# Mean and variance of the first four row tiles: ScalarE running totals replaced by VectorE statistics passes, with ten preparatory products and a new order

## The chip, the cores and the metric

The kernel runs on one core of one Trainium2 chip. The metric is device time in microseconds (us). The time before is 519.17 us, the median of three runs (518.96 to 519.18). All times of the text are us of one execution that the hardware profiler took, unless they are called run times.

## What is computed

x has 2048 rows of 512 columns, all fp32. With xn the layer norm of x along its columns:

```python
def _A_ref(x, wqkv, wo):                     # linear attention, 32 heads of 16
    q, k, v = split(x @ wqkv)
    phi = lambda t: where(t > 0, t + 1, exp(t)) + 1e-6
    kv, z = sum over rows of phi(k) v^T and of phi(k)
    return (phi(q) kv / (phi(q) z + 1e-6)) @ wo

def _B_ref(x, w1, w2, w3, w4):               # a token mixer, then an MLP of width 1376
    h = gelu(layernorm(x) @ w1)
    hs = (four column quarters of h, shifted by +1, -1, +2, -2 rows) @ w2
    x1 = x + hs
    return x1 + gelu(layernorm(x1) @ w3) @ w4

xn = layernorm(x)
out = x + _A_ref(xn, wqkv, wo) * silu(_B_ref(xn, w1, w2, w3, w4))
```

## The kernel before

The rows are 16 tiles of 128 (NT), in four blocks of four tiles (QT = 4). Most fp32 products are made on TensorE from two rounded parts of each operand, a high part (names that end in h) and the rest (names in l): three products hi*hi, lo*hi, hi*lo take the place of one. ScalarE (ACT) copies the high part, VectorE (DVE) subtracts it from the full value for the rest. A few products run in plain fp32, each as two passes: the preparatory ones (`warm`), the first chunk of the first two k tiles (`raw_k`), the column sums `ksum` and `qsum`, and the small kv and m products.

The work goes through these stages. (1) Load wk, the transposed x of block 0 (xt, u) and the four row tiles x0 to x3; make k of the tiles 0 to 3, their phi (`feature_k`: kt, kr, kNh, kNl), q of the same tiles (`query`), and the sum over rows of k times x, called g (`gram`). (2) The same for the later tiles, with the mixer of the block before between them. (3) kv and m (what attention multiplies q by). (4) The MLP, block by block: products a, pa, pb, pe, then acc, with the attention products pas, pbs, pes between, and at the end the gate and the stores.

The products of x itself do not wait for the norm: k and q are made from the raw x, and the mean is taken out afterwards with `wneg` and `qneg` (minus the column sums of the weights), the scale by rs1 = 1/sqrt(var + eps). So the mean and variance of tile i, held in `mv1`, are needed by `feature_k(i)` (the mean, in kt on VectorE), by `query(i)` (qt), and by `scale_x` (line 598): four small GpSimd (POOL) instructions w, rs (L596, a power), ns, nm, after which ACT normalises x in place (`x<-x,nm,rs`) and x is split into xNh and xNl for `gram(i)`.

How mv1 is made is `load_rows(i)` (line 1175). For tiles 4 to 15 it calls `moments` (line 588): one statistics pass of VectorE over the 512 columns (BATCH_NORM_STATS2, L590) and a short aggregate (L591). For tiles 0 to 3 it uses ACT: a copy of x with a running total (`sq<-x`), two VectorE instructions on one column that turn the total into the mean and its negative, a second ACT pass (`sq<-x,sx`, the squares of x minus the mean, with a running total), and one more VectorE instruction on one column that divides. Each running total is read out by an ACTIVATION_READ_ACCUMULATOR.

The order of the instructions on each engine isn't that of the source. `Plan` (line 86) records every operation with planned durations. `deadlines` (line 240) gives each TensorE product a nominal time and every other operation a due time, counted back from its consumers (`backward`, line 261); an operation that touches PSUM may be due no later than PATIENCE us after it could run. `nudged` (line 234) makes single operations due earlier by 0.25 times the number beside them in the table SOONER (line 1401). `emit` (line 267) then places operation after operation in a planned time line, the one that is due first among those that can go, and lets TensorE take products out of turn within `window`. Buffers come from pools: `p` with 90 tiles, `mm` and `acc` with four PSUM banks each; `lead` and `reserve` say how early an operation may take a buffer. Each engine runs its own list strictly in the planned order; where a planned time doesn't hold on the chip, the engine waits.

The helpers through which all instructions go give the line numbers of the profile: matmul L146, ACT L167, VectorE and GpSimd two-operand L189, one-operand L194, scalar-tensor-tensor L199; loads from SP L205, stores L210 and L212, fetches L217, accumulating DMAs from POOL L223. PE is TensorE, PEld its weight loads.

Of the kernel before, what the change touches and what calls it, by code (L numbers as in the profile page):

```python
# [10 lines left out]
AF = mybir.ActivationFunctionType  # L11
ALU = mybir.AluOpType
# [73 lines left out]
class Plan:  # L86
# [138 lines left out]


    GAP = .06
    PATIENCE = 2.5
    COLD, COLD_TILL = 1.84, 5.8
    SAFE = 2.0  # L230
    early = 0.0
# [8 lines left out]
    def deadlines(self, first):  # L240
# [8 lines left out]
        for op in self.ops:  # L249
# [3 lines left out]
            elif any(t.psum for t in op.tiles):  # L253
                op.due = min(op.due, op.at + self.PATIENCE)
            elif op.soon:
# [5 lines left out]
    def backward(self):  # L261
        for op in reversed(self.ops):
            if op.eng != "PE":
                for o in op.post:
                    op.due = min(op.due, o.due - self.GAP - (6.0 + op.mb * 4 if op.mb else op.lat))

    def emit(self, first, lead, reserve, window, ahead, table=()):
        self.deadlines(first)
# [125 lines left out]
def linear_attn_gated_by_mixer(  # L394
# [14 lines left out]
    S, D = x.shape  # L409
# [5 lines left out]
    QT = 4  # L415
# [3 lines left out]
    W = 4  # L419
    SHIFT = (-1, 1, -2, 2)  # L420
    ORDER = (0, 2, 1, 3)
    WARM = 8
    PIECE = BT + W
    EARLY = (), ()
    AHEAD = 30.0, 20.0, 10.0, 0.0, 0.0
# [12 lines left out]
    pl = Plan(nc, pools, counts, ("acc", "mm"))  # L438

    def piece(name, dt=F32):  # L440
        return pl.new("p", name, dt, PIECE)[:, :512]
# [8 lines left out]
    def bank(name):  # L450
        return pl.new("mm", name, F32, 512)[:, :]
# [81 lines left out]
    X, XT = {}, {}  # L533

    def load_x(i):
        X[i] = piece(f"x{i}")
        pl.load(X[i], x[i * P:(i + 1) * P, :])
# [47 lines left out]
    def small(name, n):  # L585
        return pl.new("sm", name, F32, n)

    def moments(name, xv, mv):
        st = small(name, 6).all
        pl.add("DVE", .62, .69, [xv], [st], lambda: nc.vector.bn_stats(st.get(), xv.get()))  # L590
        pl.add("DVE", .12, .2, [st], [mv], lambda: nc.vector.bn_aggr(mv.get(), st.get()))  # L591
# [576 lines left out]
    warm = bank("warm")  # L1168
    for n in range(WARM):
        pl.mm(warm.cols(n % NC * P, (n % NC + 1) * P), ones.all, ones.all, True, True, slow=True)  # L1170
# [4 lines left out]
    def load_rows(i):  # L1175
        load_x(i)
        mv = mv1[:, 2 * i:2 * i + 2]
        if i >= QT:
            moments(f"st{i}", X[i], mv)
            return  # L1180
        t, m, v = piece(f"sq{i}"), mv.cols(0, 1), mv.cols(1, 2)
        s = small(f"sx{i}", 2).all
        pl.act(t, X[i], AF.Copy, total=s.cols(0, 1))
        pl.ts(m, s.cols(0, 1), 1.0 / D, None, ALU.mult)
        pl.ts(s.cols(1, 2), s.cols(0, 1), -1.0 / D, None, ALU.mult)
        pl.act(t, X[i], AF.Square, bias=s.cols(1, 2), total=v)
        pl.ts(v, v, 1.0 / D, None, ALU.mult)

    WK = Weights("wk", wqkv[1])
    load_u(0, 2)  # L1190
# [1 line left out]
    for i in range(QT):  # L1192
        load_rows(i)
# [26 lines left out]
    query(1)  # L1220
    load_u(1, 1)
    load_rows(QT)
    scale_x(QT, 1)
    gram(1)
# [11 lines left out]
    for b in range(1, NQ):  # L1236
# [8 lines left out]
        for j in range(b == 1, QT):  # L1245
            load_rows(t0 + j)
# [50 lines left out]
    for base, s in ((0, 1), (DH - 1, -1)):  # L1297
        v = bmask.all.via(lambda ap: ap.rearrange("p (h d) -> p h d", d=DH))
# [35 lines left out]
    for b in range(NQ):  # L1334
# [46 lines left out]
        else:  # L1381
# [3 lines left out]
            t = piece(f"xi{i}", F32R)  # L1385
# [13 lines left out]
                gate(b * QT + QT - 1, a, o, D // 2, late=True, by_dma=False, whole=o > 0)  # L1399

    SOONER = (
# [6 lines left out]
    )  # L1408
    pl.emit(first=6.0, lead={"p": 14.0, "w": 14.0, "ab": 10.0}, reserve={"p": 20, "w": 1, "ab": 0}, window=12.0,
            ahead=6.0, table=SOONER)  # L1410


# [35 lines left out]
```

## Time and profile before

| | us |
|---|---|
| run time, median of three runs | 519.17 |
| run time of the profiled execution | 519.35 |
| its span, first to last instruction | 517.6 |
| PE busy | 511.2 (99%) |
| DVE busy | 394.0 (76%) |
| ACT busy | 324.8 (63%) |
| POOL busy | 102.8 (20%) |

The span is shorter than the run time by 1.75 us. Matmuls are pipelined: one of 512 columns is on record for about 0.39 us, and the next starts about 0.23 us after it, so that two overlap and the engine counts as busy without being stopped by anything. Where TensorE waits, the start of a product stands later behind the start of the one before than this step. A row of the timeline has the start, the duration, the engine, the line, the operation with output<-inputs, and the count of merged instructions; the idle time before it stands in brackets with what ended it.

### The profile page before, as it was taken

Reading aid. Unit: us, or ns where it says so; the run is one execution under the profiler, and the core shown is the slowest. Engines: PE = TensorE matmul, PEld = TensorE weight load, DVE = VectorE, ACT = ScalarE, POOL = GpSimd, SP = SyncE. Lnnn points to the kernel's source line nnn. Section 1 sums busy time; section 2 is a strip of 40 time slices with the busy share of each in tenths; the row PEclk is TensorE's granted clock in tenths of the full one; section 3 lists DMA queues with packets and bytes.
Section 4 is the critical chain, followed back from the end, with each engine's and each line's share of the span. In section 5 each row is a group of like instructions: output and inputs, shape, how many; then the busy total and the mean of one; then the engine's idle time right before and its main releaser. Section 6 shows DMA issues by size and latency. Waiting matters only on the chain.

```text
span 517.6 us, 8927 instructions
## 1 busy us (share of the span) xinstructions
PE 511.2 (99%) x3005; PEld 445.0 (86%) x3005; DVE 394.0 (76%) x788; ACT 324.8 (63%) x664; POOL 102.8 (20%) x195
## 2 busy tenths in 40 slices
PE   8999999999999999999999999999999999999996
PEld 6777888988888888898889989899898898999985
DVE  5884987569567838999999999655886657895635
ACT  5899784579558657787866755345453545535621
POOL 1378643431363022211100001000020000200000
PEclk9999999999999999999999999999999999999999
DMA  8759994375976389989767759648488376687604
GB/s 277 255 101 248 225 205 97 74 172 182 220 169 162 68 185 249 259 261 262 287 200 225 237 175 249 212 152 208 133 214 276 122 201 157 179 248 225 243 1 122
DMA packets 73281, 100.12 MB, mean 193 GB/s; under 512 B 7844, under 2 KB 30900, under 8 KB 73236
## 3 DMA queue, kind: packets, MB, share of 16 engines
q1 hardware_dynamic: 63876, 82.52, 50.6%
q0 software_dynamic: 9360, 17.04, 19.9%
q8 instruction: 23, 0.38, 0.3%
q14 instruction: 22, 0.18, 0.1%
HBM read 60.33 MB, written 30.81 MB: 176 GB/s over the span
## 4 chain that ended last, share of the span: by engine, by line
PE 91%; ACT 5%; DVE 2%; DMA 1%; issue 1%; SPq 0%; DVEq 0%
PE acc L146 22%; PE pb L146 10%; PE k L146 8%; PE h L146 8%; PE q L146 7%; PE g L146 7%; PE pe L146 5%; PE pbs L146 5%; PE pbm L146 4%; PE pa L146 3%; PE pes L146 2%; PE a L146 2%; PE pem L146 2%; PE pas L146 1%; ACT y L167 1%; PE pam L146 1%
## 5 line engine op out<-in xcount | busy, mean ns | idle before, releaser
L223 POOL DMA_DIRECT2D th<-in_x x14 | 12.2, 919 | 247.3 <-PE a L146 126.2
L167 ACT ACTIVATE p<-pb 128x256 f32<-128x256 f32 x20 | 7.7, 385 | 25.8 <-PE pb L146 25.4
L223 POOL DMA_DIRECT2D o<-x x16 | 15.0, 935 | 40.4 <-DVE o L189 19.7
L223 POOL DMA_DIRECT2D zacc<-kr x16 | 14.6, 910 | 41.8 <-DVE kr L199 33.6
L167 ACT ACTIVATE th<-xo 128x512 f32<-128x512 f32 (+1 forms) x16 | 9.7, 619 | 19.3 <-DVE xo L189 16.2
L167 ACT ACTIVATE gf<-gf 128x512 f32<-128x512 f32 (+1 forms) x40 | 20.9, 523 | 0.8
L223 POOL DMA_DIRECT2D pqd<-qe x16 | 14.7, 921 | 28.9 <-ACT p5m L167 10.0
L167 ACT ACTIVATE p<-pe 128x256 f32<-128x256 f32 x20 | 7.7, 386 | 18.9 <-PE pe L146 18.9
L189 DVE TENSOR_TENSOR xo<-acc,xo 128x512 f32<-128x512 f32 (+1 forms) x16 | 10.3, 670 | 11.4 <-PE acc L146 11.4
L199 DVE SCALAR_TENSOR_TENSOR kt<-wneg,mv,k 128x512 f32<-128x512 f32 x16 | 11.9, 742 | 9.4 <-PE k L146 8.5
L199 DVE SCALAR_TENSOR_TENSOR kr<-kt,kr 128x512 f32<-128x512 f32 x16 | 11.0, 690 | 10.4 <-ACT kt L167 10.4
L199 DVE SCALAR_TENSOR_TENSOR qt<-qneg,mv,q 128x512 f32<-128x512 f32 x16 | 11.9, 742 | 7.2 <-PE q L146 7.1
L167 ACT ACTIVATE ht<-ht 128x512 f32<-128x512 f32 x16 | 10.0, 630 | 11.5 <-DVE ht L189 11.4
L189 DVE TENSOR_TENSOR gf<-u,pe 128x256 f32<-128x256 f32 x20 | 8.3, 416 | 11.2 <-PE pe L146 11.2
L189 DVE TENSOR_TENSOR gf<-pa,p 128x256 f32<-128x256 f32 x20 | 8.4, 418 | 10.5 <-PE pa L146 10.4
L189 DVE TENSOR_TENSOR ht<-h,abc 128x512 f32<-128x512 f32 x16 | 10.8, 686 | 6.5 <-PE h L146 6.5
L167 ACT ACTIVATE x<-x,nm,rs 128x512 f32<-128x512 f32 x16 | 12.5, 802 | 2.9 <-POOL nm L189 2.9
L167 ACT ACTIVATE qr<-qt,rs 128x512 f32<-128x512 f32 x16 | 11.4, 715 | 4.1 <-DVE qt L199 4.1
L590 DVE BATCH_NORM_STATS2 st<-o 128x6 f32<-128x512 f32 x16 | 10.9, 683 | 1.8 <-DMA o<-x 1.8
L167 ACT ACTIVATE kr<-kt,rs 128x512 f32<-128x512 f32 x16 | 11.4, 715 | 1.2 <-DVE kt L199 1.1
L167 ACT ACTIVATE y<-o,nm,rs 128x512 f32<-128x512 f32 x16 | 12.0, 805 | 0.1
L167 ACT ACTIVATE kt<-kt,rs 128x512 f32<-128x512 f32 x16 | 11.4, 715 | 0.1
(1559 smaller groups left out, 2195.9 us busy)
## 6 DMA issues: line engine op xcount, KB each, us to landing
w_s<-in_w SPq DMA_DIRECT2D x28, 256.0 KB, 5.5
x<-in_x SPq DMA_DIRECT2D x16, 256.0 KB, 5.2
zacc<-kr POOLq DMA_DIRECT2D x16, 256.0 KB, 3.9
pqd<-qr SPq DMA_DIRECT2D x16, 256.0 KB, 3.3
pqd<-qe POOLq DMA_DIRECT2D x16, 256.0 KB, 5.4
o<-x POOLq DMA_DIRECT2D x16, 256.0 KB, 4.6
x1d<-o SPq DMA_DIRECT2D x16, 256.0 KB, 4.9
pq<-pqd SPq DMA_DIRECT2D x16, 256.0 KB, 6.0
```

The lines of the kernel that those rows point to most:

```text
L146: lambda: nc.tensor.matmul(out.get(), lhs.get(), rhs.get(), start=start, stop=stop, skip_group_check=more))
L167: nc.scalar.activation(out.get(), src.get(), func, scale=get(scale), **kw)
L189: self.vec(eng, out, [a, b], lambda: self.e(eng).tensor_tensor(out.get(), a.get(), b.get(), op=op), True)
L199: lambda: self.nc.vector.scalar_tensor_tensor(out.get(), a.get(), get(s), b.get(), op0=op0, op1=op1),
L223: lambda: self.nc.gpsimd.dma_start(out.get(), get(src), accum_op=ALU.add), mb=mb)
L590: pl.add("DVE", .62, .69, [xv], [st], lambda: nc.vector.bn_stats(st.get(), xv.get()))
```

## The change

`load_rows` calls `moments` for all tiles: the eight ACT passes with running totals on tiles 0 to 3 and their twelve VectorE instructions on one column go, four statistics passes and four aggregates of VectorE come. WARM, the number of preparatory products, goes from 8 to 10. The planner's parameters are changed (PATIENCE, the time that a load is due ahead, the `lead` and `reserve` of the pool p, the `window` of TensorE), and SOONER is a new table. Together they give a new order on every engine.

```diff
-    PATIENCE = 2.5
+    PATIENCE = 6.0
...
-                    op.due = min(op.due, o.due - self.GAP - (6.0 + op.mb * 4 if op.mb else op.lat))
+                    op.due = min(op.due, o.due - self.GAP - (5.0 + op.mb * 4 if op.mb else op.lat))
...
-    WARM = 8
+    WARM = 10
...
         mv = mv1[:, 2 * i:2 * i + 2]
-        if i >= QT:
-            moments(f"st{i}", X[i], mv)
-            return
-        t, m, v = piece(f"sq{i}"), mv.cols(0, 1), mv.cols(1, 2)
-        s = small(f"sx{i}", 2).all
-        pl.act(t, X[i], AF.Copy, total=s.cols(0, 1))
-        pl.ts(m, s.cols(0, 1), 1.0 / D, None, ALU.mult)
-        pl.ts(s.cols(1, 2), s.cols(0, 1), -1.0 / D, None, ALU.mult)
-        pl.act(t, X[i], AF.Square, bias=s.cols(1, 2), total=v)
-        pl.ts(v, v, 1.0 / D, None, ALU.mult)
+        moments(f"st{i}", X[i], mv)
...
     SOONER = (
-        19, 20867, 20, 10505, 21, 8920, 22, 8153, 23, 20874, 26, 12597, 28, 17, 29, 8881, 34, 1005, 35, 11144,
...
+        21, 21467, 22, 10543, 23, 8942, 24, 8165, 25, 21457, 28, 13316, 30, 56, 31, 8859, 33, 37, 36, 1010,
...
-    pl.emit(first=6.0, lead={"p": 14.0, "w": 14.0, "ab": 10.0}, reserve={"p": 20, "w": 1, "ab": 0}, window=12.0,
+    pl.emit(first=6.0, lead={"p": 12.0, "w": 14.0, "ab": 10.0}, reserve={"p": 26, "w": 1, "ab": 0}, window=9.0,
             ahead=6.0, table=SOONER)
```

What the new order does, read from the two programs side by side:

- The products are the same but for the two more `warm`, and TensorE's order differs in a few places: `qsum` follows the twelve products of q0 in place of standing before the last two; g of tile 1 follows q1 directly, where it stood behind the first four products of q2; the three products for each of g's four column groups stand together for g1 and g2; near the first mixer products (profile time 91) products of q8 stand between them; one kv product goes ahead of the first six pem products of tile 12 that follow pbm, where it stood behind the second; the m products are in three runs in place of two; in stage 4, block 0, some acc products stand elsewhere between pas, pbs, pes, pb and pe. The last 150 products are in the same order.
- SP's first two loads change places (wk ahead of the first half of xt), the last part of xt comes ahead of x0, x1 moves up by two loads, and two loads for block 1 move back.
- ACT's list at the start: u2h, wk3h, u3h, wq3h, wq0h, wq2h, the normalising of x0, wneg, wq1h, x0h, then kr and kt of the tiles 0 and 1. Before, the normalising of x0 stood seven places behind wneg.
- VectorE's list: the statistics pass of x0 follows u3l, that of x1 follows wq3l; after wneg come kt0, kt1, wq1l, the statistics of x2, wqt, kr0, wqt (the last one that `qsum` needs), x0l, k0l.
- GpSimd's four instructions for x1 follow those for x0 at once; before, an accumulating DMA stood between.

13 rows, old and new, of the table SOONER are left out of this document.

## The prediction

> **What bounds the kernel now.** First the page: busy times of the engines and the chain of waits.
>
> ```profile
> PE 511.2 (99%) x3005; PEld 445.0 (86%) x3005; DVE 394.0 (76%) x788; ACT 324.8 (63%) x664; POOL 102.8 (20%) x195
> PE 91%; ACT 5%; DVE 2%; DMA 1%; issue 1%; SPq 0%; DVEq 0%
> ```
>
> TensorE is busy for 511.2 us, 99% of the span, and 91% of the chain that ended last is its products. So only three things can move the end: when the stream of products starts, how long it stands still in between, and the tail. "Busy" hides short waits, as products overlap on record; for those I read the steps between starts in the timeline. The undisturbed step comes from the chain of waits in order of time, the waits from the timeline of TensorE:
>
> ```profile
> 37.02 2.78 PE q L146 x12
> ...
> 18.30 0.39 PE L146 MATMUL q<-wq_0h,u_0h 128*128 128x512 f32 x1
> ...
> 22.11 0.40 PE L146 MATMUL g<-k0h,x0h 128*128 128x512 f32 x1
> ...
> 25.05 0.40 PE L146 MATMUL q<-wq_0h,u_0h 128*128 128x512 f32 x1
> ...
> 28.54 0.40 PE L146 MATMUL q<-wq_1h,u_1h 128*128 128x512 f32 x1
> 29.03 0.97 PE L146 MATMUL g<-k1h,x1h 128*128 128x512 f32 x3
> 29.83 0.63 PE L146 MATMUL g<-k1l,x1h 128*128 128x512 f32 x2
> ...
> 33.53 0.39 PE L146 MATMUL q<-wq_3h,u_3l 128*128 128x512 f32 x1
> 33.94 1.20 PE L146 MATMUL g<-k2h,x2h 128*128 128x512 f32 x4
> 34.98 0.40 PE L146 MATMUL g<-k2l,x2h 128*128 128x512 f32 x1
> ```
>
> Twelve products in 2.78 us are 0.232 us each. The twelve of g0 take 25.05 - 22.11 = 2.94, so 0.16 too long. From 28.54 to 29.03 is 0.49 for one product: 0.26 of waiting, and the three behind it take 0.80 in place of 0.70. From 33.53 to 33.94 is 0.41: 0.18, and the four behind take 1.04 in place of 0.93. **In all 0.16 + 0.36 + 0.29 = 0.81 us that TensorE waits for g's operands.** The busy time by stretches says who is late there (columns: PE, PEld, DVE, ACT, POOL busy):
>
> ```profile
> 20.00:40.00 20.00, 19.88 (x82) 14.77 (x81) 16.80 (x39) 20.00 (x37) 12.08 (x22) 1.00 0.51 101
> 260.00:280.00 20.00, 19.93 (x129) 17.79 (x128) 20.00 (x44) 12.83 (x30) 0.00 (x0) 1.00 0.68 211
> ```
>
> Between 20 and 40 ACT has no free time at all; between 260 and 280 it is VectorE that has none. The first is where the change takes work away, the second is where its new order is at risk.
>
> **The change part by part.** *ACT's passes.* The grouped lines of ACT from 9 to 28 us, and for the other side the page's row of statistics passes:
>
> ```profile
> L167 ACT ACTIVATE sq<-x,sx 128x512 f32<-128x512 f32 x4 | 2.8, 708 | 0.0
> L167 ACT ACTIVATE sq<-x 128x512 f32<-128x512 f32 x4 | 2.5, 618 | 0.0
> ...
> L590 DVE BATCH_NORM_STATS2 st<-o 128x6 f32<-128x512 f32 x16 | 10.9, 683 | 1.8 <-DMA o<-x 1.8
> ```
>
> ACT loses 2.8 + 2.5 = 5.3 us and the read-outs of the totals, all of it before 28 us. VectorE gains four passes of 0.68, 2.7 us, and four aggregates, and loses twelve instructions on one column; it has 3.2 us free between 20 and 40, so this is covered, unless it stands ahead of something that TensorE needs. In the new order g1 follows q1, so TensorE comes to it at about 28.1, 0.9 us sooner than before; following the new lists with the steps of the rows (0.60 for VectorE's 512 columns, 0.52 to 0.70 for ACT's), k1h ends near 25.4, k1l near 26.1, x1l near 26.8, so there is 1.3 us to spare. For g2 (33.6) k2h ends near 30.8, k2l and x2l near 31.8. I count all 0.81 us as gone; **-0.81**. Bounds: nothing, if the operands are late again, to -0.81.
>
> *Two more preparatory products.*
>
> ```profile
> 1.12 3.78 PE L146 MATMUL warm<-ones 128*128 128x128 f32 x16 [1.12 <-POOL ones L503]
> 5.27 2.60 PE L146 MATMUL k<-wk_s,xt 128*128 128x512 f32 x4 [0.37 <-DMA wk_s<-in_wqkv]
> ...
> 225.71 2.40 PE L146 MATMUL kv<-gs,wv_s 128*128 128x128 f32 x20
> ```
>
> Each product is two passes; 16 passes take 3.78 us with the last one's drain, about 0.215 from start to start. The same kind of pass takes 2.40 / 20 = 0.12 in the kv products: TensorE starts slow and becomes fast somewhere on the way; that the four k passes, four times as wide, go in 2.60 (0.65 each with the drain, not 0.86) puts this into their time. Four more passes take 0.86 us; the stream of `warm` then ends its issue near 5.55, past the 5.27 at which wk's landing let the first k product go. So that starts 0.28 later. Until the clock opens it runs at half speed, so what it does not do in that time costs half of it later: **+0.14**, between 0 (if data are later anyway) and 0.28. The exchange of the first two loads covers nothing: both are needed for the first k product.
>
> The gate's rule is in the Trainium skill, "TensorE: Matmul & The Clock Gate", Part 1: activity is counted in windows of 3.4 us that run freely, and one busy window opens the clock. By it, filling the 0.37 us of idle time opens nothing sooner, as the window that ended in the fast clock was busy enough with that gap. The rows agree with an opening within these four passes; where the windows lie in a run no row here can show.
>
> *The wait that is added.* In ACT's new list the normalising of x0 stands ahead of wneg, and it waits for GpSimd's nm of x0. Behind it in ACT's queue are wneg, wq1h and all of kr and kt; VectorE's kt0, wq1l and the last wqt wait for these, TensorE's `qsum` for that.
>
> ```profile
> 13.08 0.25 POOL L194 TENSOR_SCALAR w<-mv 128x1 f32<-128x1 f32 x1 [10.02 <-DVE mv L194]
> ...
> 15.22 0.47 POOL L189 TENSOR_TENSOR nm<-mv,ns 128x1 f32<-128x1 f32 x1
> ...
> 15.73 0.60 ACT L167 ACTIVATE wneg<-ksum 128x512 f32<-128x512 f32 x1 [1.58 <-PE ksum L146]
> ...
> 16.36 0.75 DVE L199 SCALAR_TENSOR_TENSOR kt<-wneg,mv,k 128x512 f32<-128x512 f32 x1 [0.72 <-ACT wneg L167]
> ```
>
> The chain on GpSimd takes 15.22 + 0.47 - 13.08 = 2.61. It started when mv was there, at 13.08. In VectorE's new list one pass (0.68) more stands ahead of that mv, but half a pass (u0l) and three short instructions fewer, and the load that u3 needs comes sooner: mv near 13.1 again, nm near 15.7. Normalising x0 then holds ACT for 0.70, wneg goes from 15.73 to 16.4, and kt0 from 16.36 to 17.0. Then VectorE has kt0, kt1 (0.66 each), wq1l, a statistics pass, wqt, kr0 (0.60 each) and the last wqt, which ends at 21.4. q0 starts at 18.30 + 0.14 and its twelve products end at 21.2, and `qsum` waits: **+0.25**. If GpSimd is as quick as its fastest rows, nothing; if mv is there one pass later, +0.9. I take the rows' own times.
>
> *Later places.* TensorE's other waits of that kind, from the timeline:
>
> ```profile
> 221.59 0.28 PE L146 MATMUL pbm<-w_t2h,hs23l 128*128 128x256 f32 x1
> 222.15 0.38 PE L146 MATMUL pem<-w_b22h,hs43h 128*128 128x256 f32 x1 [0.28 <-ACT p5m L167]
> ...
> 262.83 0.40 PE L146 MATMUL acc<-w_1l,f_1h 128*128 128x512 f32 x1
> 263.30 0.39 PE L146 MATMUL pb<-yt40h,w_b 128*128 128x256 f32 x1
> ```
>
> At 221.59 one product of 256 columns (step 0.12) takes 0.56: 0.44 of waiting for ACT's p5m. In the new order a kv product, two passes of 0.12, fills half of it; a third run of m products, with another change between fp32 and rounded products, gives some 0.1 back: **-0.1**. At 262.83 it waits 0.47 - 0.23 = 0.24 for VectorE; there the pass ahead is the same in the new list, and the wait stays: 0. The other moves (loads, buffers, the filling of stage 4 with acc products) go past engines that have time: cost 0. If that cover is gone, one VectorE pass (0.68) at each such place is the price. The tail has the same order: 0.
>
> **Sum:** -0.81 + 0.14 + 0.25 - 0.1 = -0.52. Against the profiled run's 519.35 that is 518.83; that run was 0.18 above the median, so against 519.17 it is **518.65, and I say 518.7**.
>
> **Rivals.** *All the waits go (faster).* For: ACT has over 5.3 us less, and the order is free to use it everywhere. Then `qsum` doesn't wait (-0.25), the rest of p5m's wait (-0.34) and that at 262.83 (-0.24) go: -0.52 - 0.83 = -1.35, **517.8**.
>
> *The change does nothing.* ACT's free time lies behind the normalising of x0, which is in order ahead of everything; the waits for g move from ACT's load to GpSimd's chain. Then only half of the 0.81 is gained, and 0.14 and 0.25 are paid: **519.2**. Against it: 1.3 us to spare at g1.
>
> *VectorE sets the pace in stage 4 (slower).* From 260 to 280 it is busy for 20.00 of 20.00 us, and with the new order the evacuation of pa in pair 3 stands some fifteen places later. In block 0 five pairs of pb products wait for VectorE; if each waits a whole pass (0.68) where the one at 262.83 waits 0.24, that is 5 x 0.44 = 2.2 us, on top of -0.52: 519.17 + 1.7 = **520.9**. It decides from the point at which a pass that TensorE needs stands more than some 0.5 us later in VectorE's list. Against it: TensorE has acc products to fill with, and the work of VectorE ahead of these evacuations is about the same in both lists.
>
> *The clock opens elsewhere.* If the slow time lasts longer by as much as the 16 preparatory passes took (3.8 us), half of that is lost: 519.17 + 1.9 - 0.5 = 520.6; if it ends before the first k product, the four k passes take 4 x 0.43 and gain some 0.7: 518.0. The page of the Trainium skill named above would let it, as its windows run freely. Against it: the three runs lie within 0.22 us.
>
> **How the numbers follow.** The forecast has 0.44, all waits gone 0.24, nothing 0.18, VectorE's pace 0.11, the clock 0.03. The forecast's own range is 518.2 to 519.2. The range reaches to the first rival and towards the third: 517.5 to 520.1. 0.2% (1.04 us, about what a measurement of this kernel can tell from no change) puts the borders at 518.13 and 520.21. Faster: 0.22 of the first rival, 0.06 of the forecast, 0.02 of the clock: 0.30. Slower: 0.11 and 0.02: 0.13. The same: 0.57.
>
> **What would show it.** In the profile after: no `sq` rows; TensorE's step at the start of g1 and g2 without a gap (right), or a gap at `qsum` above 0.5 us (wrong: the added wait is dearer); the first k product at 5.5 (not 5.27); wneg at 16.4, behind x0's normalising. q1 should start near 25.3 (now 25.05) and g1 near 28.1 (now 29.03). Past 45 us the steps should have the same small gaps as before; a sum of new ones above 1 us between 240 and 320 would make the prediction wrong, as would a start that moves by more than 0.5 us.

## The result, and the profile after

The changed kernel takes 523.25 us (median of four runs, 522.75 to 523.61) against 519.17 before: the ratio is 1.0075, 95% interval 1.0063 to 1.0087. It is slower by 4.1 us, where 518.7 (517.5 to 520.1) was forecast. Its profiled execution took 523.61, with a span of 521.9.

The page of the changed kernel, busy times and chain of waits:

```profile
PE 512.9 (98%) x3009; PEld 447.2 (86%) x3009; DVE 395.1 (76%) x784; ACT 321.7 (62%) x650; POOL 101.4 (19%) x195
...
PE 79%; DVE 7%; ACT 5%; DMA 5%; issue 2%; SPq 1%; POOL 0%; DVEq 0%; ACTq 0%
```

VectorE has gained 1.1 us, as the edit says. ACT has lost only 3.1, though the passes that went were 5.3 and their read-outs came on top: the new order has ten instructions ACT_TABLE_LOAD on ACT in place of eight, 1.28 us each; two of them, at 91.71 and 93.65, stand around a single `qe`. No step of TensorE between 90 and 100 us is over 0.3, so they are not the loss. TensorE is busy for only 1.7 us more, but the span is 4.3 longer, and TensorE's share of the chain has fallen from 91% to 79%; VectorE's and the DMAs' have grown. Somewhere TensorE stands still behind a load and VectorE. The starts of certain products in the two timelines say where (us between them):

| stretch of TensorE's list | before | after | difference |
|---|---|---|---|
| start to the first split product, k<-wk_0h,u_0h | 7.30 | 6.83 | -0.47 |
| from there to the transpose ab of block 0 | 37.91 | 37.94 | +0.03 |
| to the mixer's first product h | 31.28 | 36.23 | **+4.95** |
| to the MLP's first product a | 159.47 | 159.73 | +0.26 |
| to the end of the last product | 277.15 | 276.63 | -0.52 |
| to the span's end | 4.53 | 4.54 | +0.01 |

One stretch holds the whole loss. In it there is one place, between the products g6 and g7 (g of the tiles 6 and 7); TensorE's timeline, first of the kernel before, then of the changed kernel:

```profile
73.47 0.39 PE L146 MATMUL g<-k6h,x6l 128*128 128x512 f32 x1
73.71 0.63 PE L146 MATMUL g<-k7h,x7h 128*128 128x512 f32 x2
```

```profile
73.02 0.39 PE L146 MATMUL g<-k6h,x6l 128*128 128x512 f32 x1
76.06 0.50 PE L146 MATMUL g<-k7h,x7h 128*128 128x512 f32 x1 [2.65 <-ACT k7h L167]
76.78 0.50 PE L146 MATMUL g<-k7l,x7h 128*128 128x512 f32 x1 [0.22 <-DVE k7l L199]
77.12 0.57 PE L146 MATMUL g<-k7h,x7l 128*128 128x512 f32 x1
...
80.04 0.63 PE L146 MATMUL g<-k7h,x7h 128*128 128x512 f32 x1
80.47 0.46 PE L146 MATMUL g<-k7l,x7h 128*128 128x512 f32 x1
80.76 0.39 PE L146 MATMUL g<-k7h,x7l 128*128 128x512 f32 x1
```

The undisturbed step is 0.23. From 73.02 to 76.06 are 3.04: 2.81 of waiting for k7h. To 76.78 are 0.72: 0.49 of waiting for k7l. Then no operand is on record as late, and still the steps are longer, 0.43 each from 77.48 to 80.47; the ten up to 80.76 take 3.98 in place of 2.30 and cost another 1.68. In all 4.98. What the slow steps are stands in the table by stretches of the changed kernel (the last three columns are granted clock, DMA share and GB/s):

```profile
74.00:77.18 3.18, 0.90 (x3) 0.54 (x4) 3.12 (x6) 3.03 (x6) 0.36 (x1) 1.00 0.00 0
77.18:80.60 3.42, 3.42 (x10) 2.68 (x9) 1.44 (x3) 2.80 (x4) 3.09 (x12) 0.50 0.81 141
80.60:84.00 3.40, 3.40 (x16) 2.74 (x15) 0.00 (x0) 0.00 (x0) 1.06 (x7) 1.00 1.07 275
```

The granted clock is 0.50 for 3.41 us from 77.18 on, 1.1 us after the long wait ended, and 1.00 again after it. It is no chance of this profile: the mean granted clock is 0.995 or 0.996 in all four executions of the changed kernel, and 0.999 or 1.000 in all four of a_fill below, which has no idle time there.

k7h comes from kt of tile 7, a VectorE instruction. VectorE's timeline (its kt rows and the first sum of the mixer's second weight, `w_f<-w_s,w_s`), first of the changed kernel, then of the one before:

```profile
50.76 0.75 DVE L199 SCALAR_TENSOR_TENSOR kt<-wneg,mv,k 128x512 f32<-128x512 f32 x1 [0.94 <-PE k L146]
56.48 0.69 DVE L189 TENSOR_TENSOR w_f<-w_s,w_s 128x512 f32<-128x512 f32 x1 [4.98 <-DMA w_s<-in_w]
...
71.57 0.74 DVE L199 SCALAR_TENSOR_TENSOR kt<-wneg,mv,k 128x512 f32<-128x512 f32 x1
```

```profile
53.20 0.68 DVE L189 TENSOR_TENSOR w_f<-w_s,w_s 128x512 f32<-128x512 f32 x1
...
68.73 0.74 DVE L199 SCALAR_TENSOR_TENSOR kt<-wneg,mv,k 128x512 f32<-128x512 f32 x1
```

**VectorE stands for 4.98 us, from 51.5 to 56.48, behind a sum from which TensorE needs nothing before 97.8**, because the sum's operand is still under way. Qt5, kr5, k5l, x6l and all up to kt7 queue behind it; kt7 comes 2.84 later than before, and TensorE's hole is 2.81. Why the operand is late starts in SP's list; SP's timeline after, then before:

```profile
37.37 0.88 SPq L205 DMA_DIRECT2D w_s<-in_w  x2
41.46 0.33 SPq L210 DMA_DIRECT2D pqd<-qr  x1
41.88 4.37 SPq L205 DMA_DIRECT2D w_s<-in_w  x6
```

```profile
36.78 2.41 SPq L205 DMA_DIRECT2D w_s<-in_w  x4
39.28 3.27 SPq L210 DMA_DIRECT2D pqd<-qr  x2
42.65 2.77 SPq L205 DMA_DIRECT2D w_s<-in_w  x4
```

Before, w1's four loads go ahead of the two stores of qr. After, a store that waits for ACT's qr3 until 41.46 has two of them behind it, and w2's four behind those. The second load of w2, the one the sum waits for, is issued at nearly the same time (43.69 after, 43.41 before), but with two more loads freshly ahead of it: it lands at 56.39 in place of 52.87, 12.7 us after its issue in place of 9.5. These are the longest times to landing among the loads of `w_s`, after, then before:

```profile
DMA to landing us min/median/max: 7.4/9.2/12.7
DMA to landing us min/median/max: 5.3/8.8/9.5
```

Whether the two loads ahead explain the 3.2 us more is tested below (b_loads_late, a_gather_late).

### The profile page after: what moved, and what is told of

Same layout as the page of the kernel before. It is cut to its first block, busy times and chain, and to the rows that moved or that the text cites. A ratio compares the mean times of both kernels' runs of the same rounds, so it can differ in the third digit from the quotient of the medians.

```text
span 521.9 us, 8869 instructions
## 1 busy us (share of the span) xinstructions
PE 512.9 (98%) x3009; PEld 447.2 (86%) x3009; DVE 395.1 (76%) x784; ACT 321.7 (62%) x650; POOL 101.4 (19%) x195
## 4 chain that ended last, share of the span: by engine, by line
PE 79%; DVE 7%; ACT 5%; DMA 5%; issue 2%; SPq 1%; POOL 0%; DVEq 0%; ACTq 0%
PE acc L146 23%; PE pb L146 11%; PE h L146 6%; PE pe L146 6%; PE pbs L146 4%; PE k L146 4%; PE g L146 4%; PE q L146 4%; PE pbm L146 4%; PE pa L146 3%; DMA w_s<-in_w 2%; PE pes L146 2%; PE a L146 2%; PE pem L146 2%; DMA o<-x 2%
## 5 line engine op out<-in xcount | busy, mean ns | idle before, releaser
L223 POOL DMA_DIRECT2D pqd<-qe x16 | 16.4, 1027 | 33.8 <-ACT qe L167 22.4
```

Source lines behind the costliest of these rows:

```text
L223: lambda: self.nc.gpsimd.dma_start(out.get(), get(src), accum_op=ALU.add), mb=mb)
```

## The experiments

In the kernels below the planned lists are kept as they are but for the places shown, unless it is said that the planner solved anew; the code that moves the places shifts line numbers by one or more. Each diff is of an engine's list.

**a_loads_first**, the changed kernel, SP's list:

```diff
 w_s (w1, 2 loads)
-pqd<-qr3
 w_s (w1, 2 loads)
 w_s (w2, 4 loads)
+pqd<-qr3
```

> The changed kernel with one store elsewhere in SP's list: the store of qr3, which waited for ACT until 41.46 with six weight loads behind it, stands behind these loads. Theory 'late load': the last load that the first sum needs is issued near 39.7 in place of 43.69 and lands up to 4 us sooner than 56.4 (it took 12.7 us with the DMA engines full, so perhaps only 2 sooner); VectorE's wait of 4.98 falls to 1 to 3 us, and TensorE's hole at 73.02 to under 1: 518.5 to 520. Theory 'head of the queue' alone (the load can't be sooner as the DMA engines are full): wait and hole stay, 523.

518.78 (518.55 to 520.78), ratio to before 0.9997 (0.9988 to 1.0007). VectorE's row of the sum and TensorE's step from g6 to g7:

```profile
53.14 0.69 DVE L190 TENSOR_TENSOR w_f<-w_s,w_s 128x512 f32<-128x512 f32 x1 [1.28 <-DMA w_s<-in_w]
```

```profile
73.38 0.39 PE L147 MATMUL g<-k6h,x6l 128*128 128x512 f32 x1
73.60 0.40 PE L147 MATMUL g<-k7h,x7h 128*128 128x512 f32 x1
```

The wait falls to 1.28, the hole is gone, and with it the whole loss: in the changed kernel the place of this one store in SP's queue is enough to make the loss or to take it away. The load was hardly quicker (issued at 40.78, landed after 12.3 us in place of 12.7); it came in time because it was issued 2.9 us sooner. What is left of the change is then no faster than before either.

**a_sum_late**, the changed kernel, VectorE's list:

```diff
-w_f<-w_s,w_s
 qt5
 kr5
-w_f<-w_s,w_f
 k5l
 x6l
+w_f<-w_s,w_s
+w_f<-w_s,w_f
```

> The changed kernel with two VectorE instructions elsewhere in the list and nothing else: the first two sums of the mixer's second weight (w_f<-w_s,w_s and w_f<-w_s,w_f) stand behind x6l. In the changed kernel VectorE stood 4.98 us (51.5 to 56.48) at the first of them for a load, kt of tile 7 came at 71.57 (68.73 before), and TensorE's first product with k7 at 76.06 where the one ahead of it started at 73.02. Theory 'head of the queue': qt5, kr5, k5l and x6l go while the load is under way, everything up to kt7 comes about 2.9 us sooner, k7h near 72.5, and the hole at 73.02 shrinks from 2.81 to under 0.5; slow steps behind it (0.43 in place of 0.23) go too: 523.25 - 4.6 = 518.6. Rival 'too much work': VectorE has the same instructions ahead of kt7 and they simply don't fit; then the order of two of them changes nothing: 523.2.

520.36, ratio 1.0016 (1.0007 to 1.0026): missed. VectorE's rows and TensorE's:

```profile
57.30 0.69 DVE L190 TENSOR_TENSOR w_f<-w_s,w_s 128x512 f32<-128x512 f32 x1
...
69.87 0.75 DVE L200 SCALAR_TENSOR_TENSOR kt<-wneg,mv,k 128x512 f32<-128x512 f32 x1
```

```profile
74.37 0.50 PE L147 MATMUL g<-k7h,x7h 128*128 128x512 f32 x1 [0.55 <-ACT k7h L168]
```

The sum no longer waits, but VectorE gains only 1.7 us at kt7 (69.87 in place of 71.57), not 2.9: four instructions are too few to fill the wait, as qt5 itself waits for its products until 53.94. A hole of 0.71 + 0.49 remains. So the sum's place at the head of the queue is a part of the loss, not all of it; the 16 instructions from w_t4l to w_2l stand between the sums and kt7 in either list.

**a_gather_late**, the changed kernel, GpSimd's list:

```diff
-pqd<-qe3
 ...
 zacc<-kr (the next)
+pqd<-qe3
```

> The changed kernel with one accumulating DMA of GpSimd elsewhere: pqd<-qe of tile 3, issued at 47.45 in the changed kernel, stands behind the next zacc<-kr (55.25); SP's list and VectorE's are as in the changed kernel. The load that VectorE stood for was issued at 43.69 and took 12.7 us; in the kernel before with the loads late it was issued at 44.39 and took 9.4, with two accumulating DMAs between 41 and 49 in place of four. Theory 'GpSimd's accumulations slow the load': it lands 1 to 2.5 us sooner than 56.4, VectorE's wait falls from 4.98 to 2.5 to 4, TensorE's hole from 2.81 to 0.5 to 2: 520.5 to 522.5. Rival 'only SP's list matters': wait, hole and time stay, 523.

520.56, ratio 1.0019 (1.0010 to 1.0029), as the first theory has it. The load is issued at 43.70, as before this move, and lands after 10.9 us in place of 12.7:

```profile
54.70 0.69 DVE L190 TENSOR_TENSOR w_f<-w_s,w_s 128x512 f32<-128x512 f32 x1 [3.20 <-DMA w_s<-in_w]
```

```profile
74.28 0.50 PE L147 MATMUL g<-k7h,x7h 128*128 128x512 f32 x1 [0.89 <-ACT k7h L168]
```

So an accumulating DMA of GpSimd that is issued beside a load of SP can make that load later. With these runs there is a dose and a response: VectorE's wait of 4.98, 3.20 and 1.28 gives kt7 at 71.57, 69.78 and 68.57, and a hole of 2.81, 1.04 and none. From the first to the second each us of wait is a us of hole; carried on, that line has no hole left at a wait of about 2.2, which is an estimate. And the hole of 1.04 closes no clock: behind the wait for k7l, g7's steps are 0.23.

**a_fill**, the changed kernel with 13 products of ones, of two passes each, between g6 and g7; nothing else is changed.

> The changed kernel with 13 products of ones by ones (128 columns, two passes of 0.118 us each, so 3.07 us) put into the hole between g6 and g7; their results are overwritten. They don't bring k7 sooner: g7 starts near 76.3 as k7l is there at 76.7. Theory 'clock': the 12 products of g7 take 0.43 each in the changed kernel because the hole of 2.81 us closed the fast clock (the record shows 0.5 for 3.41 us); with the hole filled they take 0.23, and 1.7 us come back: 521.5. Rival: the slow steps come from late operands or DMA traffic, not from the idle time: 523.2.

521.80, ratio 1.0046 (1.0033 to 1.0060): 1.45 less than the changed kernel. TensorE's timeline:

```profile
73.31 3.06 PE L435 MATMUL h<-ones 128*128 128x128 f32 x26
76.12 0.48 PE L147 MATMUL g<-k7h,x7h 128*128 128x512 f32 x1
76.44 0.39 PE L147 MATMUL g<-k7l,x7h 128*128 128x512 f32 x1
76.67 0.39 PE L147 MATMUL g<-k7h,x7l 128*128 128x512 f32 x1
```

G7 starts no sooner (76.12), but its steps are 0.23 from its second product on. The slow steps came from the idle time, not from late operands.

**b_loads_late**, the kernel before, SP's list:

```diff
 w_s (w1, 2 loads)
-w_s (w1, 2 loads)
 pqd<-qr2
 pqd<-qr3
+w_s (w1, 2 loads)
 w_s (w2, 4 loads)
```

> The kernel before with SP's list as in the changed kernel at one place: the last two of w1's four loads stand behind the stores of qr2 and qr3 in place of ahead of them; no other difference on any engine. Before, qr3's store went at 42.22 and w2's first loads at 42.65 and 43.41, 8.2 and 9.5 us to landing. Theory 'late load': the second load that the first sum needs is issued near 44.4 behind two more loads and lands near 56 to 57, VectorE waits 3 to 4 us at w_f<-w_s,w_s, kt7 comes at 71 to 72 (68.73 before), a hole of 2 to 3 us opens between g6 and g7, with slow steps behind it if it closes the clock: 522 to 524. Rival 'VectorE's order and the rest of the new order': before's list stands the late load and nothing of this comes: 519.2 to 519.7.

520.18, ratio 1.0021 (1.0007 to 1.0034): slower, but by a quarter of what was expected.

```profile
53.84 0.69 DVE L190 TENSOR_TENSOR w_f<-w_s,w_s 128x512 f32<-128x512 f32 x1 [0.56 <-DMA w_s<-in_w]
```

```profile
74.20 0.73 PE L147 MATMUL g<-k7h,x7h 128*128 128x512 f32 x2 [0.34 <-ACT k7h L168]
```

Here the load was issued at 44.39 and landed after 9.4 us, with the same two loads freshly ahead of it; so these two are not what made it slow. Three of GpSimd's accumulations were issued between 41 and 49 us (w1t's is one), in place of four in the changed kernel. VectorE came to the sum at 53.28, not at 51.5 as there, and waited 0.56 and then 1.15 for ACT's k5h; the hole is 0.50, with 0.16 at the next product. The order of SP's list gives a hole in the old kernel too; its size in the new one needs the slower load and VectorE's earlier arrival as well. Why the load is slower there is shown in part (1.8 us by a_gather_late): the DMA engines as a whole are no busier (share 1.01 between 41 and 57 us, 1.05 here).

**b_warm**, the kernel before with two more preparatory products (ten) and its order kept.

> The kernel before with two more preparatory products (10 in place of 8) and no other difference, no order changed. My prediction's term: the first k product 0.28 later, +0.14, so 519.3. Theory 'no gap': in the changed kernel the first k product starts at 5.51 but the four raw passes go in 0.43 each, where before the first two took 0.98 and 0.60 after a gap of 0.37; the split products start at 6.83 in place of 7.30. If the two products alone do that, it shows here: 6.83, and 519.17 - 0.47 = 518.7. Rival 'exchange of loads': it was the first two loads changing places; then the split products start at 7.3 to 7.6 here and the time is 519.2 to 519.4.

519.47, ratio 0.9997 (0.9987 to 1.0007): no difference that this interval, from -0.7 to +0.4 us, can show.

```profile
5.54 2.34 PE L147 MATMUL k<-wk_s,xt 128*128 128x512 f32 x4
7.32 0.80 PE L147 MATMUL k<-wk_0h,u_0h 128*128 128x512 f32 x1
```

The raw k product starts 0.27 later, as forecast, and the split ones at 7.32 in place of 7.30, not at 6.83 as the "no gap" theory has it; my +0.14 is too small to be settled here. The exchange of loads isn't it either, as other executions of the changed order have their split products at 7.61 and 7.71; the last section says what it is.

**b_stats**, the kernel before with the edit of the heading alone: ACT's passes and the one-column instructions are left out, a statistics pass and aggregate stand where the first one-column instruction of each tile stood. **b_stats_again** is the same once more.

> The kernel before with the edit of the heading alone and its order kept on every engine: the eight ScalarE passes with running totals go; VectorE's statistics pass and aggregate of each of the four tiles stand where the first of that tile's one-column instructions stood. Theory 'as forecast': ACT has 5.3 us less up to 28 us, the waits of TensorE at g0, g1 and g2 (0.16, 0.36 and 0.29) go, 518.4 to 518.6. Rival 'VectorE is the late one there': the four passes of 0.68 stand ahead of k's and x's parts in a list that was full from 20 to 30 us (9.55 of 10), the waits move to VectorE and stay or grow: 519.2 to 520.

> The run with the edit of the heading alone a second time, one look: in its profiled execution TensorE waited 1.14 at 483.91 (0.17 before), as VectorE waited 1.61 for a DMA of attention's q. Theory 'chance of that execution': 0.17 here, and the waits at k, qsum and g0 as before (0.37, 0.40, 0.53, 0.23): 520.2 to 520.5. Rival: the edit makes that load late, 1.1 again: 521.3.

520.51, ratio 1.0028 (1.0017 to 1.0040), and 520.26: above even the rival's 519.2 to 520. The waits at g1 and g2 went, as forecast, but others came (b_stats_again):

```profile
21.24 1.12 PE L147 MATMUL qsum<-wqt,ones 128*128 128x512 f32 x2 [0.24 <-DVE wqt L190]
```

The rival holds: VectorE is the late one. Beside 0.40 at `qsum` there are 0.53 and 0.23 at g0 for k0l and x0l. The wait of 1.14 at 483.91 was a chance of the first execution (0.16 in the second), and so was 0.37 for u3l at 13.28.

**b_stats_place**, the same with the passes placed by hand in VectorE's list:

```diff
 u_3l
+statistics of x0
 ...
 wq_2l
+statistics of x1
 ...
 k0l
-kt2
 x0l
+statistics of x2
+kt2
+statistics of x3
 kt3
```

> The kernel before with the edit of the heading (statistics passes for the first four tiles, no ScalarE totals), as in the run with that edit alone, but with the passes at other places of VectorE's list: x0's behind u3l, x1's behind wq2l, x2's and x3's behind x0l, kt2 between them. With the edit alone TensorE waited 0.37 for u3l in k (13.28), 0.40 at qsum, 0.53 and 0.23 at g0. Theory 'place in VectorE's list': the same four passes cost nothing to k and g0 from there; 0.37 + 0.76 come back, qsum's wait stays: 519.2 to 519.5, no difference from before. Rival 'VectorE is full': whatever stands behind is late in its turn, and the waits move to g1, g2 or q1: 520 to 520.6.

520.60, ratio 1.0021 (1.0012 to 1.0031): the rival again.

```profile
21.50 1.12 PE L147 MATMUL qsum<-wqt,ones 128*128 128x512 f32 x2 [0.47 <-DVE wqt L190]
...
30.69 0.96 PE L147 MATMUL g<-k1h,x1h 128*128 128x512 f32 x3 [1.12 <-ACT x1h L168]
```

```profile
29.40 0.72 ACT L168 ACTIVATE k1h<-kr,tiny 128x512 fp32r<-128x512 f32 x1 [2.50 <-DVE kr L200]
```

G0 has no wait now, but `qsum` has 0.63 and g1 has 1.28. X1's mean is not late (x1 is normalised at 26.10, before at 27.04); ACT's x1h stands behind k1h, and k1h waits 2.50 for VectorE's kr. With the old order of the rest, the edit in the heading costs 1.1 to 1.5 us by these ratios, in both places that were tried.

**a_le**, the changed kernel with `lead` of the pool p at 14 again; the planner solved anew.

> The changed kernel with one planner parameter put back: buffers of the pool p may be taken 14 us ahead again in place of 12; the planner solves the order anew, so some 140 places of TensorE's list and 350 of VectorE's differ. In its SP list all four w1 loads and no store stand otherwise than before: two loads ahead of qr2's store, two ahead of qr3's. Theory 'late load, from the shorter lead': no stand of VectorE above 1.5 us at w_f, no hole above 0.5 us between g6 and g7: 518.3 to 519.8. Rival 'the table of nudges and the parameters fit only together': a stand or hole elsewhere, 520 or more.

523.46, ratio 1.0082 (1.0068 to 1.0096). The hole at g7 is gone; new waits came between 80 and 140 us, of which TensorE's table of waits has this as the largest (in total, times, longest), and the MLP takes 1.4 longer than before:

```profile
PE pbm L146 <- ACT p1m L167: 0.9, 1, 0.9
```

The rival holds: parameter and table fit only together, and one alone tells nothing about its own worth. Which of the parameters put the store ahead of the loads is therefore left open.

**a_best** and **a_win**, the changed kernel with a_loads_first's move and one more each:

```diff
 a_best, VectorE's list
-statistics of x2
 wqt
 kr0
 wqt (the last)
+statistics of x2
 a_win, ACT's list
-gs2
-gs3
 p1m
+gs2
+gs3
 zb
-yb210h
 p5m
+yb210h
```

> The changed kernel with two moves: the store of qr3 behind the six weight loads, and VectorE's statistics pass of x2 behind the last wqt in place of ahead of the two. Theory: the store's move takes away the hole at 73 (518.78 with it alone); the second move brings the last wqt from 21.4 to 20.8, so that qsum, which waited 0.42 in the changed kernel, doesn't wait: another 0.3 to 0.45, 518.3 to 518.5, faster than before by 0.1 to 0.2%. Rival: x2's statistics or kt2 are late in their turn, and what qsum gains is lost at g2 or k2: 518.8 to 519.2.

> The changed kernel with the store of qr3 behind the six weight loads (as in the run with that move alone, 518.78) and two moves in ScalarE's list near 220 us: p1m ahead of the last two gs<-g copies, p5m ahead of yb210h. In that run TensorE waited 0.46 for p1m between pem and pbm (221.12), and 0.33 for p5m ahead of pem (222.63). Theory: both waits go, 0.6 to 0.8 us less, 518.0 to 518.3, faster than before by 0.2%. Rival: ScalarE is then late for zb or y's parts, and TensorE waits for those (a<-yb110h at 236.74 or pb behind it): 518.6 to 519.

519.03, ratio 0.9998 (0.9989 to 1.0007), and 519.25, ratio 1.0000 (0.9991 to 1.0009): no gain in either, as the rivals have it.

```profile
23.03 0.50 PE L147 MATMUL g<-k0l,x0h 128*128 128x512 f32 x1 [0.20 <-DVE k0l L200]
```

```profile
223.13 0.39 PE L147 MATMUL pbm<-w_t3h,hs33h 128*128 128x256 f32 x1 [0.34 <-ACT u2m L168]
```

In a_best `qsum`'s wait falls from 0.42 to 0.21, and k0l, on time in the changed kernel, is waited for; between pem and pbm, near 221, the wait for p1m is 0.85 where a_loads_first has 0.46. In a_win the waits for p1m and p5m go, and u2m is the next. No version here beats the kernel before.

## Why the prediction was wrong

The opening, by its own marks, in the changed kernel's timeline of TensorE, ACT's row of wneg and VectorE's of the last wqt:

```profile
5.51 1.89 PE L146 MATMUL k<-wk_s,xt 128*128 128x512 f32 x4
6.83 0.79 PE L146 MATMUL k<-wk_0h,u_0h 128*128 128x512 f32 x1
...
21.49 1.13 PE L146 MATMUL qsum<-wqt,ones 128*128 128x512 f32 x2 [0.26 <-DVE wqt L189]
...
25.25 0.39 PE L146 MATMUL q<-wq_0h,u_0h 128*128 128x512 f32 x1
...
28.04 0.39 PE L146 MATMUL g<-k1h,x1h 128*128 128x512 f32 x1
```

```profile
16.42 0.58 ACT L167 ACTIVATE wneg<-ksum 128x512 f32<-128x512 f32 x1
```

```profile
20.75 0.68 DVE L189 TENSOR_TENSOR wqt<-wqt,wq_s 128x512 f32<-128x512 f32 x1
```

- **What bounds the kernel**: right. TensorE's stream decides, and its stops add up to the result.
- **Waits for g's operands, -0.81**: right. Before g1 and g2 no step is long (g1 at 28.04, forecast 28.1).
- **Two more preparatory products, +0.14**: the start at 5.51 is as forecast; the cost stays open, as b_warm shows no difference but could not show one so small.
- **The added wait, +0.25**: wneg at 16.42 (16.4), the last wqt ends at 21.43 (21.4), so the list was followed rightly. But `qsum` waits 0.42, and the steps of q0 hold another 0.43 that I left out, 0.33 of it at the products with wq_1: they wait for wq_1l, which stands behind kt0 and kt1 in the same list. Both grow by what q0 starts sooner (17.83, not 18.44).
- The sum of these to the transpose ab was -0.42; it measured -0.44, of which -0.47 lies ahead of the first split product and is chance, as the last section shows: the number came out by luck. In this execution the order gained nothing from there on: what g no longer waits, q0 and `qsum` do. In a_loads_first and a_sum_late the split products start later (7.71 and 7.61), and the same stretch takes 37.42 and 37.57 in place of 37.91, so there the order did gain up to 0.5.
- **p5m, -0.1**: the wait fell as far as that (0.33 in place of 0.44), but the 0.1 for the third run of m products had no row behind it: the change of product type costs 0.40 there, so the term came out near +0.3.
- **Later places, cost 0**: this is the step that failed. "The other moves (loads, buffers, the filling of stage 4 with acc products) go past engines that have time: cost 0." For stage 4 that was even too dear (-0.52). For the loads it was wrong by +4.95: I followed each moved load to its consumer as far as 45 us, and took the rest of SP's list as free. There two loads, and four more behind them, had gone behind a store, and an engine "with time", VectorE, has an order. Its busy time between 50 and 55 us is 0.75 of 5 in the changed kernel and 3.83 before: that idle time was the damage, not slack. The price I named if the cover failed, one pass of 0.68, was wrong in kind: the wait in the queue was 4.98 long and became a hole of 2.81, and behind it came the clock with 1.68.
- **The rivals**: the slower one had VectorE as the late engine, with 520.9, in stage 4; nothing of it came there. "The clock opens elsewhere" I held against by three run times within 0.22 us; the clock records show that it opens elsewhere in every execution. In this one it opened at 5.50, ahead of the first k product, as in that rival's fast case; its gain of 0.7 did not come (-0.44 at ab), and run times close together say nothing against it.
- **What would show it**: the sign that failed is "past 45 us the steps should have the same small gaps as before". I set a limit for their sum only between 240 and 320 us; the hole lay at 73.

## What to carry to other kernels

In a planned order, a load goes no sooner than what stands ahead of it in its queue: for each load that moves past a store or an accumulation, ask what that one waits for, when the load then lands on busy DMA engines, and which engine's queue comes to a stand for it. An instruction that is needed late but stands early is harmless only while its operand is early: list for each in-order engine the instructions whose operands come by DMA, and count what queues behind. A hole in TensorE's stream costs its length and can cost slow clock on top (here 2.81 and 1.68 us; the hole of 1.04 cost only itself): where operands can't come sooner, fill it, which gave 1.45 back here.

## What the runs showed of the hardware

The clock records say when TensorE's full clock begins in each profiled execution: 4.35 us after the span's start in b_stats, 4.50, 4.94, 5.39, 5.50 (the changed kernel), 5.93, 5.98, 6.46, 6.57 (the kernel before), 6.64, 6.84, 7.08, 7.28, and 7.32 in b_stats_place. It doesn't go by kernel: b_stats and b_stats_again are the same program, 4.35 and 6.84. The first split product follows between 6.74 (4.35) and 7.71 (7.28), so up to 1 us of its start is chance, and a difference of 0.5 in one profile's first 8 us tells nothing. Not all of it lasts: in b_stats and b_stats_again the first split product starts at 6.74 and 7.50, the transpose ab at 45.90 and 45.89. The lengths of the stretches at full clock are 508.59, 512.00 or 515.41 us, and 71.68 and 440.32 in the changed kernel: 149, 150, 151, 21 and 129 times 3.413. So the clock is decided in windows of 3.41 us whose phase the kernel doesn't set. The Trainium skill, "TensorE: Matmul & The Clock Gate", Part 1, says that the activity window runs freely and that the number of slow products varies from run to run with its phase; the records agree.

The window that closed the clock, 73.77 to 77.18, was not empty: TensorE had no product in it until 76.06, 2.29 of 3.41 us, and it is on record as busy for 0.90. That page of the Trainium skill gives an idle window as the condition; here one that was idle for more than two thirds was enough, while the hole of 1.04 in a_gather_late closed nothing. The ends of the kernels narrow it down: in the kernel before the clock closed at 515.16 behind a window in which TensorE was busy for 1.36 us, and in b_warm it stayed open behind one with 1.58 (511.63 to 515.05). So the border, if there is one, lies between 40% and 46% of a window by these records.

The load of 256 KB that VectorE's sum waits for took 9.4 to 12.7 us to land in these runs; moving one accumulation of GpSimd out of its way took 1.8 us off. The Trainium skill, "DMA: Bandwidth & Descriptors", Queues, rings and completion order, has each DMA engine take turns among the queues that have work, packet by packet; the 1.8 us agree with it.
